# Block-sparse attention and MLP mixer on one core: the last batch's second MLP layer as seven block products

## The chip, the core and the metric

The kernel runs on one core of a Trainium2 chip. The metric is device time of one execution in microseconds: 278.38 us is the median of 9 runs of the kernel before (277.9 to 279.4). The work is shared between TensorE (PE, matrix products, with its weight loads shown as PEld), VectorE (DVE), ScalarE (ACT), GpSimd (POOL) and the DMA queues, of which SyncE (SP) issues most. The accumulators of PE lie in PSUM[...]; here they are handed out as "doubles", tiles of two banks.

## The reference, cut to what matters

For 4 batches of 768 rows, block-sparse attention of 8 heads of 64 gives x, and a mixer follows:

```
h = xt @ U @ V                      # over the sequence, rank 32
u = x + h.transpose(0, 2, 1)
ch = np.maximum(u @ w_ch1, 0.0) @ w_ch2
return (u + ch).astype(np.float32)
```

u is 768 x 512 for each batch, w_ch1 512 x 2048, w_ch2 2048 x 512. The change touches the last product, `@ w_ch2`, of the last batch alone.

## The kernel before, in words

The first batch's attention is done head pair by head pair. From then on a planner written into the kernel interleaves two streams for PE: attention units of the next batches (`try_unit`, `try_values`, `try_a`, `try_h`) and the MLP of a finished batch, held as a queue of small steps (`fill`, made by `mlp_steps(b)`, lines 717 to 888). The planner keeps a clock for each engine (`clk`), with durations written in by hand, and a list of tasks for ACT and DVE (`later`, `run_engines`). Nothing of it runs on the chip: it decides the order in which each engine's instructions stand, and each engine works its list strictly in that order, with semaphores between the engines.

For the last batch (b = 3) no attention is left to be interleaved. Its u, transposed (`uTs[b]`), comes from a chain for the last head pair: the values' product `pav`, DVE normalises it (`rcp`, `xs`, lines 588 and 590), POOL casts it (`xh`, 599), PE `pa`, DVE `a` (628, 629), PE `ph`, DVE `xf` (676), POOL `uh` (685), and a transposing DMA on SP (`uT`, 695). Meanwhile PE still works on the second layer of batch 2 (`w2_rows`), which DVE adds to `xf` and sends (`leave`, 792 and 795).

Then the last batch's MLP runs alone:

- **First layer** (`w1`, line 771). For each of 16 blocks jj of 128 hidden channels, 8 matmuls of 384 columns fill one double `pt`, and ACT's ReLU (line 737) writes it as fp16 into the tile `tT[jj]` (128 channels x 768 positions).
- **Second layer** (`w2`, line 826). For each of 6 row tiles sc, 16 matmuls of 512 columns accumulate over jj; stationary is `tT[jj][:, sc*128:...]`, moving is `w2t[:, jj, :]`. The last row tile is cut in columns 0 to 383 and 384 to 511. `leave` adds the bank to `xf` on DVE into a tile `of`, and SP sends it.

Positions are laid out with the six row tiles t as p*6+t, so "upper half" below means row tiles 0 to 2 and "lower half" 3 to 5. `double()` (line 114) gives out the double that comes free first; from line 1140 on there are four (numbers 0 to 3). Every matmul is issued at line 173 (`mm`).

Of the kernel before, what the change touches and what calls it, by code (L numbers as in the profile page):

```python
# [10 lines left out]
FP32 = mybir.dt.float32  # L11
FP16 = mybir.dt.float16
# [9 lines left out]
def kernel(  # L22
# [91 lines left out]
    def double(name, n=None):  # L114
        if n is None:
            n = min(doubles, key=lambda n: doubles[n][1])
            assert doubles[n][1] < OPEN
            clk["pe"] = max(clk["pe"], doubles[n][1])
        pool = doubles[n][0]
        t = pool.tile([P, 2, 512], FP32, tag=f"double{n}", name=name)  # L120
        doubles[n] = (pool, OPEN)
        held[id(t)] = (n, t)
        return t

    def give_back(t, when):
        n = held.pop(id(t))[0]
        doubles[n] = (doubles[n][0], when + LAG)
# [6 lines left out]
    def later(eng, first, fn, when=None):  # L134
        count[0] += 1
        when = clk["pe"] if when is None else when
        tasks[eng].append((when + LAG, first, count[0], fn))

    def run_engines(t):
        while True:  # L140
            best = None
            for eng in ("act", "dve"):
                for kind in (eng, "any"):
                    for task in tasks[kind]:
                        start = max(clk[eng], task[0])
                        late = 0.15 if kind == "any" and eng == "dve" else 0.0
                        key = (start + late, task[1], task[2])
                        if start <= t and (best is None or key < best[0]):
                            best = (key, eng, kind, task, start)
            if best is None:  # L150
                return
            _, eng, kind, task, start = best
            tasks[kind].remove(task)
            clk[eng] = start
            clk[eng] += task[3](eng)

    def more_doubles(tag, n):
        first[tag].__exit__(None, None, None)
        pool = ctx.enter_context(
            tc.tile_pool(  # L160
                name=f"double{n}p", bufs=1, space=bass.MemoryType.PSUM,
                side="left" if tag == "ps" else "right",
            )
        )
        doubles[n] = (pool, clk["pe"])

    def run_on(eng, us, ready=None):
        clk[eng] = max(clk[eng], (clk["pe"] if ready is None else ready) + LAG) + us
# [2 lines left out]
    def mm(out, lhsT, rhs, start, stop, loose=False, us=0.0):  # L171
        clk["pe"] += us
        ins = nc.tensor.matmul(  # L173
            out, lhsT, rhs, start=start, stop=stop, skip_group_check=loose
        )
        keep(ins)
        return ins
# [536 lines left out]
        run_on("dve", 0.6)  # L714


    def mlp_steps(b):
        tT = {}
        steps = []
# [5 lines left out]
        def relu(tiles, pt):  # L725
            if tiles[0][0] == tiles[1][0]:
                outs = [(tile_of(tiles[0][0]).rearrange("p (c n) -> p c n", c=2), pt[:, :, 0:HS])]
            else:
                outs = [
                    (tile_of(jj)[:, c * HS : (c + 1) * HS], pt[:, n, 0:HS])  # L730
                    for n, (jj, c) in enumerate(tiles)
                ]

            def run(eng):
                for o, i in outs:
                    if eng == "act":
                        keep(nc.scalar.activation(out=o, in_=i, func=AF.Relu))  # L737
                    else:
                        keep(nc.vector.tensor_scalar_max(out=o, in0=i, scalar1=0.0))  # L739
                us = {"act": 0.81, "dve": 0.95}[eng] + 0.16 * (len(outs) - 1)  # L740
                give_back(pt, clk[eng] + us)
                return us

            later("any", 1, run)

        def tile_of(jj):
            if jj not in tT:
                tT[jj] = tpool.tile([P, S], FP16, tag="tT", name="tT")
            return tT[jj]

        def w1_rows(key, tiles, phase, cc0=0, cc1=NCC):

# [32 lines left out]
        def leave(sc, nsc, n0, n1, pch, whole):  # L785
            if sc % 2 == 0 and n0 == 0:
                pair["of"] = opool.tile([P, 2, HD], FP32, tag="of", name="of")
            of = pair["of"][:, sc % 2 : sc % 2 + nsc, n0:n1]

            def run(eng):  # L790
                keep(
                    nc.vector.tensor_add(out=of, in0=xfs[b][:, sc : sc + nsc, n0:n1], in1=pch)  # L792
                )
                keep(
                    nc.sync.dma_start(
                        out=out[b].rearrange("(p t) d -> p t d", t=T)[:, sc : sc + nsc, n0:n1],
                        in_=of,
                    )
                )
                us = 0.1 + 0.55 * nsc  # L800
                give_back(whole, clk["dve"] + us)
                return us

            later("dve", 2, run)
# [18 lines left out]
            if phase == 1 and part == 7:  # L823
                leave(s0, 2, 0, HD, pair["pch"], pair["pch"])

        def w2(sc, part, n0, n1):
            if part == 0:
                pair["pch"] = double("pch")
            pch = pair["pch"][:, 0:1, 0 : n1 - n0]
            for jj in range(4 * part, 4 * part + 4):  # L830
                mm(
                    pch[:, 0, :],
                    tT[jj][:, sc * P : (sc + 1) * P],
                    w2t[:, jj, n0:n1],
                    jj == 0, jj == NJJ - 1, us=0.217 * (n1 - n0) / HD,
                )
            if part == 3:
                leave(sc, 1, n0, n1, pch, pair["pch"])

        rowed = b < B - 1  # L840
        if b == 0:

            first = [[(2 * k, 0), (2 * k + 1, 0)] for k in range(2)]
            for k, phase, cc0 in (
# [8 lines left out]
                        "",  # L853
                    )
                )
        for jj in range(NJJ):
            tiles = [(jj, 0), (jj, 1)]
            if b == 0 and jj < 4:
                if jj % 2:
                    continue  # L860
                tiles = [(jj, 1), (jj + 1, 1)]
            for ph in range(2):
                if rowed:
                    fn = lambda jj=jj, tiles=tiles, ph=ph: w1_rows(jj, tiles, ph)
                else:
                    fn = lambda jj=jj, ph=ph: w1(jj, ph)
                kind = "open" if ph == 0 else "swap" if rowed else ""
                steps.append((0.65, fn, kind))
        if rowed:
# [5 lines left out]
                            (0.434, lambda s0=s0, ph=ph, part=part: w2_rows(s0, ph, part), kind)  # L875
                        )
            return steps
        for sc in range(T):
            for n0, n1 in [(0, HD)] if sc < T - 1 else [(0, 384), (384, HD)]:
                for part in range(4):  # L880
                    steps.append(
                        (
                            0.87 * (n1 - n0) / HD,
                            lambda sc=sc, part=part, n0=n0, n1=n1: w2(sc, part, n0, n1),
                            "" if part else "open",
                        )
                    )
        return steps

    def start_batch(b):  # L890
# [190 lines left out]
    def next_unit(held_back=False):  # L1081
        i, u = stream.popleft()
        est = new_est()
        ests_of.setdefault(i, []).append(est)
        state["out"] += 1

        def mask(eng):
            us = mask_mul(u, est)
            masked.setdefault(i, []).append(clk["dve"] + us)
            return us  # L1090

        if held_back:
            scores(i, u, est)
            early.append(mask)
        else:
            scores(i, u, est, mask)
        unit_sides(i, u)
# [86 lines left out]
    def rate():  # L1184
# [4 lines left out]
            return max(left - 11.0, 0.0) / units if units else 1.2  # L1189
        return max(left - 12.9, 0.0) / max(units, 1)  # L1190

    def try_unit(due):
        if not stream or state["out"] > 12 or not free_double():
            return False
        if clk["act"] > clk["pe"] + (0.36 if due else 1.0) or due and credit < rate():
            return False
        next_unit()
        return True

    def try_fill():  # L1200
# [9 lines left out]
    while stream or fill or do_v or do_a or do_h or opened < B:  # L1210
        run_engines(clk["pe"])
        if not fill and opened < B and len(uT_at[opened]) == HP:
            if max(uT_at[opened]) <= clk["pe"]:
                fill.extend(mlp_steps(opened))
                opened += 1
        if try_h() or try_a() or try_values():
            continue
        if try_unit(True):
            credit -= rate()
            continue  # L1220
        if try_fill():

            weight = 0.87 if fill[0][0] > 0.5 else 1.24
            credit = min(credit + weight * run_fill(), 3.0)
            continue
        if try_unit(False):
            credit -= rate()
            continue
        clk["pe"] += 0.05
# [31 lines left out]
```

The softmax here doesn't subtract the row's maximum and nothing guards it: scores larger than these inputs give would overflow.

## Time and profile before

| | before |
|---|---|
| median of 9 runs | 278.38 us |
| the profiled execution, its own time | 278.47 us |
| its span in the profile | 276.7 us |
| PE busy | 270.7 us (98%) |
| DVE / ACT / POOL busy | 175.2 / 177.0 / 103.2 us |
| last batch, first layer on PE | 232.10 to about 252.9 us |
| last batch, second layer on PE | 252.91 to 273.83 us |
| last DVE addition starts | 273.88 us |

The span is what lies between the first and the last instruction of the profiled execution; its own time is 1.77 us longer. In the timeline view each row is a group of like instructions: start, duration, engine, line, operation, tile written and tiles read, shape, count, and in brackets the idle time of the engine before it with what ended it. Matmuls of one group overlap in the array, so the distance from one to the next is the group's duration less one instruction's mean, divided by the count less one. In the windows view each row is a stretch of time with the busy time of each engine in it, the granted TensorE clock (1.00 is full), the busy share of DMA and the GB/s.

### The profile page before, as it was taken

How to read it: one execution, taken by the hardware profiler on the slowest of the kernel's cores; microseconds unless marked ns; L12 is line 12 of the kernel's file. 1: busy time of each engine (PE TensorE's matmuls, PEld its weight loads, DVE VectorE, ACT ScalarE, POOL GpSimd, SP SyncE). 2: the span in 40 equal slices, each digit the busy share in tenths (PEclk: the TensorE clock that was granted, in tenths of full speed). 3: DMA queues.
4: the chain of work that ended last, by engine and by line, in shares of the span. 5: the costliest groups of instructions: out<-in, count | busy, mean ns of one | idle time of the engine just before them, and what ended most of it. 6: DMA issues, size and time to landing. Idle time of an engine off the chain costs nothing.

```text
span 276.7 us, 8037 instructions
## 1 busy us (share of the span) xinstructions
PE 270.7 (98%) x3493; PEld 161.9 (59%) x3493; DVE 175.2 (63%) x286; ACT 177.0 (64%) x198; POOL 103.2 (37%) x137
## 2 busy tenths in 40 slices
PE   8999999999999999999999999999999999999995
PEld 2677775565656564656565565656565654655443
DVE  6777758878797987777756768777777451000112
ACT  4899995877897857694955749584886201664000
POOL 4768639407274835363604536361102020000000
PEclk9999999999999999999999999999999999999999
DMA  6999957999979999995990989995100322000222
GB/s 192 310 297 263 281 136 104 182 181 77 136 48 118 168 121 145 155 108 71 49 123 0 189 91 161 136 98 75 31 2 2 104 79 81 25 1 0 78 77 76
DMA packets 85484, 31.65 MB, mean 114 GB/s; under 512 B 75152, under 2 KB 83048, under 8 KB 85448
## 3 DMA queue, kind: packets, MB, share of 16 engines
q0 software_dynamic: 49824, 10.29, 43.0%
q1 hardware_dynamic: 35268, 20.62, 33.4%
q8 instruction: 27, 0.44, 0.7%
q10 hardware_dynamic: 356, 0.22, 0.3%
q14 instruction: 9, 0.07, 0.1%
HBM read 27.84 MB, written 6.29 MB: 123 GB/s over the span
## 4 chain that ended last, share of the span: by engine, by line
PE 82%; ACT 11%; DMA 2%; DVE 1%; POOL 1%; issue 1%; SPq 0%; DVEq 0%; POOLq 0%
PE pch L173 30%; PE pt L173 30%; ACT est L499 11%; PE pav L173 10%; PE psc L173 9%; DMA kld<-in_k_dram 2%; PE pa L173 2%; PE ph L173 1%; POOL xh L599 0%; DVE xh L542 0%; DVE xs L590 0%; POOL qst L247 0%; POOL kst L327 0%; PE puT L704 0%; DVE uT L713 0%
## 5 line engine op out<-in xcount | busy, mean ns | idle before, releaser
L499 ACT ACTIVATE est<-psc 128x1024 f16<-128x1024 f32 x144 | 143.0, 1028 | 46.0 <-PE psc L173 44.6
L173 PE MATMUL pt<-uT,w1t 64*128 64x384 f16 (+1 forms) x896 | 94.4, 324 | 0.0
L173 PE MATMUL pch<-w2t,tT 64*128 64x512 f16 (+3 forms) x688 | 93.6, 372 | 0.1
L520 DVE TENSOR_TENSOR est<-est,m 128x1024 f16<-128x1024 f16 x108 | 78.3, 740 | 18.2 <-ACT est L499 16.8
L173 PEld LDWEIGHTS <-w1t 64*128 64x128 f16 (+1 forms) x896 | 46.0, 95 | 36.2 <-PE pt L173 8.4
L173 PEld LDWEIGHTS <-tT 64*128 64x128 f16 (+1 forms) x688 | 38.2, 95 | 36.9 <-PE pch L173 1.6
L737 ACT ACTIVATE tT<-pt 128x768 f16<-128x768 f32 (+1 forms) x48 | 36.6, 773 | 26.0 <-PE pt L173 26.0
L173 PEld LDWEIGHTS <-est 128*128 128x128 f16 x1152 | 41.4, 97 | 10.9 <-issue 5.0
L173 PE MATMUL pav<-vt,est 128*128 128x65 f16 x1152 | 44.5, 193 | 0.1
L792 DVE TENSOR_TENSOR of<-xf,pch 128x1024 f32<-128x1024 f32 (+3 forms) x16 | 15.2, 950 | 42.7 <-PE pch L173 42.7
L173 PE MATMUL psc<-qT,kT 64*128 64x512 f16 (+1 forms) x288 | 40.6, 323 | 0.3 <-ACT est L499 0.3
L599 POOL CAST xh<-xs 128x768 f16<-128x768 f32 x12 | 10.4, 870 | 79.8 <-DVE xs L590 74.2
L685 POOL CAST uh<-xf 128x768 f16<-128x768 f32 x12 | 13.9, 1161 | 26.1 <-DVE xf L676 14.5
L173 PE MATMUL psc<-qa,ka 128*128 128x512 f16 (+1 forms) x96 | 21.5, 326 | 0.6 <-ACT est L499 0.4
L739 DVE TENSOR_SCALAR tT<-pt 128x768 f16<-128x768 f32 (+1 forms) x20 | 18.3, 917 | 5.9 <-PE pt L173 5.8
L173 PEld LDWEIGHTS <-kT 64*128 64x128 f16 x288 | 14.6, 94 | 12.5 <-issue 0.7
L261 POOL DMA_DIRECT2D vt<-in_v_dram x20 | 16.3, 820 | 3.1 <-DMA w2t<-in_moe_w_ch_dram 3.1
L261 POOL DMA_DIRECT2D qst<-in_q_dram x20 | 16.3, 819 | 0.1
L261 POOL DMA_DIRECT2D kst<-in_k_dram x20 | 16.3, 820 | 0.0
L590 DVE TENSOR_TENSOR xs<-pav,rcp 128x768 f32<-128x768 f32 x12 | 11.5, 958 | 1.2
L676 DVE TENSOR_TENSOR xf<-xs,ph 128x768 f32<-128x768 f32 x12 | 11.4, 951 | 1.2 <-PE ph L173 1.2
L173 PEld LDWEIGHTS <-ka 128*128 128x128 f16 (+1 forms) x108 | 8.8, 97 | 3.6 <-issue 1.8
(70 smaller groups left out, 130.8 us busy)
## 6 DMA issues: line engine op xcount, KB each, us to landing
out_dram<-of SPq DMA_DIRECT2D x9, 512.0 KB, 3.3
vld<-in_v_dram SPq DMA_DIRECT2D x6, 384.0 KB, 7.2
w1t<-in_moe_w_ch_dram POOLq DMA_DIRECT2D x4, 512.0 KB, 9.0
w2t<-in_moe_w_ch_dram POOLq DMA_DIRECT2D x4, 512.0 KB, 10.0
qld<-in_q_dram SPq DMA_DIRECT2D x5, 384.0 KB, 6.6
kld<-in_k_dram SPq DMA_DIRECT2D x5, 384.0 KB, 8.0
qst<-in_q_dram POOLq DMA_DIRECT2D x20, 96.0 KB, 4.2
kst<-in_k_dram POOLq DMA_DIRECT2D x20, 96.0 KB, 4.4
```

What stands on the lines that cost most here:

```text
L173: ins = nc.tensor.matmul(out, lhsT, rhs, start=start, stop=stop, skip_group_check=loose)
L261: keep(nc.gpsimd.dma_start(out=o[:, h], in_=src_of(nm, i)[:, h]))
L499: keep(nc.scalar.activation(out=est, in_=psc, func=AF.Exp, scale=0.125))
L520: keep(nc.vector.tensor_tensor(out=o, in0=o, in1=m, op=ALU.mult))
L590: nc.vector.tensor_tensor(out=xs.rearrange("p (c j) (h d) -> p c (j h) d", c=2, h=2), in0=pv[:, :, :, 0:D], in1=rcp[:, :, :, None].broadca ...
L599: keep(nc.gpsimd.tensor_copy(out=xh, in_=xs))
L676: nc.vector.tensor_tensor(out=u.rearrange("p (c j) n -> p c j n", c=2), in0=xs.rearrange("p (c j) n -> p c j n", c=2), in1=ph[:, :, 0:HS]. ...
L685: keep(nc.gpsimd.tensor_copy(out=uh, in_=u))
L737: keep(nc.scalar.activation(out=o, in_=i, func=AF.Relu))
L739: keep(nc.vector.tensor_scalar_max(out=o, in0=i, scalar1=0.0))
L792: nc.vector.tensor_add(out=of, in0=xfs[b][:, sc : sc + nsc, n0:n1], in1=pch)
```

## The change

The second layer of the last batch becomes a Strassen product. The hidden activations t (768 x 2048) are cut in four blocks by upper and lower half of the positions and by jj 0 to 7 and 8 to 15; w_ch2 is cut by the same jj and by columns 0 to 255 and 256 to 511. With A the blocks of t and B those of w_ch2:

```
P1=(A11+A22)(B11+B22)  P2=(A21+A22)B11  P3=A11(B12-B22)  P4=A22(B21-B11)
P5=(A11+A12)B22        P6=(A21-A11)(B11+B12)             P7=(A12-A22)(B21+B22)
C12 = P5+P3    C21 = P2+P4    C22 = P1-P2+P3+P6    C11 = P1+P4-P5+P7
```

For each of three groups g of 128 positions in either half, each product is 8 matmuls of 256 columns.

- **Weight sums** (`add_w2`): ten DVE additions in fp16, five of 128x1536 and five of 128x512, put into the lists of DVE as soon as the last attention unit is issued, with the lowest priority (9). They are written into old load tiles and into `qa`.
- **Activation sums** (`add_t`): after the ReLU of jj+8, four DVE operations in fp16 (one of 768, three of 384 elements), eight times. Two of the four write in place over `tT`. The order of the first layer is changed to jj = 0, 8, 1, 9, ...
- **PSUM**: before the last batch's MLP is queued, doubles 2 and 3 are given up and become four tiles of one bank (`split_double`). The first layer is left with doubles 0 and 1.
- **Products** (`w2_product`): order P3, P5, P4, P2, P1, P6, P7. P3 and P5 fill the halves of tile `pa`, P4 and P2 those of `pb`, P1 lies in `pc`. P6 is accumulated onto P3, and P7 onto P4, after DVE has read P3 and P4 once. In the last group P7 is cut in two pieces of 128 columns, the second in `pd`.
- **Leaving**: DVE adds into `xf` in place, in pieces of 256 columns (three additions for `pa`, three for `pb`, one of 2x256 for `pc`, one each for P6 and P7 in a group), and SP sends 11 pieces of 128x256 and two of 128x128 in place of five of 128x512, one of 128x384 and one of 128x128.

How the planner orders this in the built program: on DVE four weight sums stand ahead of the last head pair's `rcp`, three between `xs` and `a`, and three behind `xf`; the last pair's `pa` stands 4 matmuls of the second layer of batch 2 later, and its `ph` 12 later. All 16 ReLUs of the last batch stay on ACT. First-layer tiles alternate between doubles 1 and 0; in every group `pa` is taken in double 1, `pb` in double 0, `pc` in one and the same single bank, and in the last group `pd` in a second; two single banks stay unused. The lists of ACT and POOL are the same as before; that of SP differs only in the output pieces.

The core of the diff:

```diff
+    def bank(name):
+        free = [(at, n) for n, (_, at) in banks.items()]
+        free += [(at + 0.1, n) for n, (_, at) in doubles.items()]
+        at, n = min(free, key=lambda f: (max(f[0], clk["pe"]), str(f[1])))
...
+            for o, i0, i1, op in (
+                (both, lo, hi, ALU.add),
+                (diag, lo[:, 0:HS], hi[:, HS:S], ALU.add),
+                (lo[:, HS:S], lo[:, HS:S], lo[:, 0:HS], ALU.subtract),
+                (hi[:, 0:HS], hi[:, 0:HS], hi[:, HS:S], ALU.subtract),
+            ):
+                keep(nc.vector.tensor_tensor(out=o, in0=i0, in1=i1, op=op))
...
+        def w2_product(g, n, j0, j1, n0=0, n1=HB):
+            where = {3: ("a", 0), 5: ("a", HB), 4: ("b", 0), 2: ("b", HB), 1: ("c", 0),
+                     6: ("a", 0), 7: ("b", 0)}
...
+                mm(
+                    o, t_sum[n, j][:, g * P : (g + 1) * P], w[:, n0:n1],
+                    fresh and j == 0, j == NJ - 1, True, us=0.108 * (n1 - n0) / HB,
+                )
...
+                if n == 5:
+                    acc(c11, pt[:, HB:512], ALU.subtract)
+                    acc(c12, pt[:, HB:512])
+                    acc(c12, pt[:, 0:HB])
+                    send(c12)
+                    done.add("a")
...
-        def w2(sc, part, n0, n1):
-            if part == 0:
-                pair["pch"] = double("pch")
-            pch = pair["pch"][:, 0:1, 0 : n1 - n0]
-            for jj in range(4 * part, 4 * part + 4):
-                mm(
-                    pch[:, 0, :],
-                    tT[jj][:, sc * P : (sc + 1) * P],
-                    w2t[:, jj, n0:n1],
-                    jj == 0, jj == NJJ - 1, us=0.217 * (n1 - n0) / HD,
-                )
-            if part == 3:
-                leave(sc, 1, n0, n1, pch, pair["pch"])
...
+        for g in range(3):
+            for n in (3, 5, 4, 2, 1, 6, 7):
+                for n0, n1 in [(0, HB)] if (g, n) != (2, 7) else [(0, P), (P, HB)]:
+                    for j0 in range(0, NJ, 4):
...
+                if opened == B - 1:
+                    while max(doubles[n][1] for n in (2, 3)) >= OPEN:
+                        clk["pe"] += 0.05
+                        run_engines(clk["pe"])
+                    for n in (2, 3):
+                        split_double(n)
```

More of the change, by code (lines that the diff above doesn't have):

```diff
@@ L158, in more_doubles @@
         first[tag].__exit__(None, None, None)
-        pool = ctx.enter_context(
+        closing[n] = ctx.enter_context(ExitStack())
+        pool = closing[n].enter_context(
             tc.tile_pool(
@@ L165, in more_doubles, with split_double, bank_back @@
         doubles[n] = (pool, clk["pe"])
+    closing, banks = {}, {}
+    def split_double(n):
+        assert doubles[n][1] < OPEN
+        at = doubles.pop(n)[1]
+        closing[n].close()
+        pool = ctx.enter_context(
+            tc.tile_pool(
+                name=f"bank{n}p", bufs=1, space=bass.MemoryType.PSUM,
+                side="left" if n == 3 else "right",
+            )
+        )
+        for m in range(2):
+            banks[f"bank{n}{m}"] = (pool, at)
+    def bank(name):
+        free = [(at, n) for n, (_, at) in banks.items()]
+        free += [(at + 0.1, n) for n, (_, at) in doubles.items()]
+        at, n = min(free, key=lambda f: (max(f[0], clk["pe"]), str(f[1])))
+        while min(banks.get(n, doubles.get(n))[1], OPEN) == OPEN:
+            clk["pe"] += 0.05
+            run_engines(clk["pe"])
+            free = [(at, n) for n, (_, at) in banks.items()]
+            free += [(at + 0.1, n) for n, (_, at) in doubles.items()]
+            at, n = min(free, key=lambda f: (max(f[0], clk["pe"]), str(f[1])))
+        if n in doubles:
+            clk["pe"] = max(clk["pe"], doubles[n][1])
+            return double(name, n)[:, 0, :], n
+        pool, at = banks[n]
+        clk["pe"] = max(clk["pe"], at)
+        banks[n] = (pool, OPEN)
+        return pool.tile([P, 512], FP32, tag=n, name=name), n
+    def bank_back(n, when):
+        if n in doubles:
+            for k in [k for k, v in held.items() if v[0] == n]:
+                del held[k]
+            doubles[n] = (doubles[n][0], when + LAG)
+        else:
+            banks[n] = (banks[n][0], when + LAG)
     def run_on(eng, us, ready=None):
@@ L714, in turn_u_pe, with w2_block, add_w2 @@
         run_on("dve", 0.6)
+    NJ, HB = NJJ // 2, HD // 2
+    W_SUMS = {
+        "11+22": (0, 0, 1, 1, ALU.add),
+        "12-22": (0, 1, 1, 1, ALU.subtract),
+        "21-11": (1, 0, 0, 0, ALU.subtract),
+        "11+12": (0, 0, 0, 1, ALU.add),
+        "21+22": (1, 0, 1, 1, ALU.add),
+    }
+    w_sum = {}
+    def w2_block(x, y, j0, j1):
+        return w2t[:, x * NJ + j0 : x * NJ + j1, y * HB : (y + 1) * HB]
+    def add_w2(n):
+        k, part = n // 2, n % 2
+        key = list(W_SUMS)[k]
+        x0, y0, x1, y1, op = W_SUMS[key]
+        if n == 0:
+            for m in range(6):
+                t = ldpool.tile([P, 6, HB], FP16, tag="ld" + "qkv"[m % 3], name="w2s")
+                w_sum["home", m] = t
+        j0, j1 = ((0, 6), (6, NJ))[part]
+        if part == 0:
+            o = w_sum["home", k][:, 0:6, :]
+        elif k < 3:
+            o = w_sum["home", 5][:, 2 * k : 2 * k + 2, :]
+        else:
+            o = qa[0][k - 3].rearrange("p (j n) -> p j n", n=HB)[:, 0:2, :]
+        keep(
+            nc.vector.tensor_tensor(
+                out=o, in0=w2_block(x0, y0, j0, j1), in1=w2_block(x1, y1, j0, j1), op=op
+            )
+        )
+        for j in range(j0, j1):
+            w_sum[key, j] = o[:, j - j0, :]
+        return 1.12 if part == 0 else 0.42
     def mlp_steps(b):
@@ L741, in run @@
                 give_back(pt, clk[eng] + us)
+                if not rowed:
+                    jj = tiles[0][0]
+                    full.add(jj)
+                    if (jj + NJ) % NJJ in full:
+                        later("dve", 1, lambda e: add_t(jj % NJ), clk[eng] + us)
                 return us
@@ L749, in tile_of, with add_t @@
             return tT[jj]
+        rowed = b < B - 1
+        full, t_sum, added = set(), {}, set()
+        def add_t(j):
+            lo, hi = tT[j], tT[NJ + j]
+            if j % 2 == 0:
+                t_sum["two"] = new_est().rearrange("p a n -> p (a n)")
+            both = new_est().rearrange("p a n -> p (a n)")[:, 0:S]
+            diag = t_sum["two"][:, (j % 2) * HS : (j % 2 + 1) * HS]
+            for o, i0, i1, op in (
[5 more added lines that the diff above has]
+                keep(nc.vector.tensor_tensor(out=o, in0=i0, in1=i1, op=op))
+            t_sum[1, j] = diag
+            t_sum[2, j] = both[:, HS:S]
+            t_sum[3, j] = lo[:, 0:HS]
+            t_sum[4, j] = hi[:, HS:S]
+            t_sum[5, j] = both[:, 0:HS]
+            t_sum[6, j] = lo[:, HS:S]
+            t_sum[7, j] = hi[:, 0:HS]
+            added.add(j)
+            return 1.5
@@ new lines, in force, with acc, send, run @@
+        def force(done):
+            while not done():
+                clk["pe"] += 0.05
+                run_engines(clk["pe"])
+        def w2_product(g, n, j0, j1, n0=0, n1=HB):
+            where = {3: ("a", 0), 5: ("a", HB), 4: ("b", 0), 2: ("b", HB), 1: ("c", 0),
+                     6: ("a", 0), 7: ("b", 0)}
+            nm, at = where[n] if n0 == 0 else ("d", 0)
+            fresh = n in (3, 4, 1) or nm == "d"
+            if j0 == 0:
+                if fresh:
+                    pair[nm, g] = bank("p" + nm)
+                if n == 3:
+                    pair["done", g] = set()
+            done = pair["done", g]
+            if n in (6, 7) and j0 == 0 and nm != "d":
+                force(lambda: nm in done)
+            o = pair[nm, g][0][:, at : at + n1 - n0]
+            for j in range(j0, j1):
+                force(lambda: j in added and ("21+22", NJ - 1) in w_sum)
+                w = {
+                    1: lambda: w_sum["11+22", j],
+                    2: lambda: w2_block(0, 0, j, j + 1)[:, 0, :],
+                    3: lambda: w_sum["12-22", j],
+                    4: lambda: w_sum["21-11", j],
+                    5: lambda: w2_block(1, 1, j, j + 1)[:, 0, :],
+                    6: lambda: w_sum["11+12", j],
+                    7: lambda: w_sum["21+22", j],
+                }[n]()
+                mm(
+                    o, t_sum[n, j][:, g * P : (g + 1) * P], w[:, n0:n1],
+                    fresh and j == 0, j == NJ - 1, True, us=0.108 * (n1 - n0) / HB,
+                )
+            if j1 < NJ:
+                return
+            last = g == 2
+            xq = xfs[b].rearrange("p t (c n) -> p (t c) n", c=2)
+            c11, c12, c21, c22 = 2 * g, 2 * g + 1, 2 * g + 6, 2 * g + 7
+            def acc(q, i, op=ALU.add, n0=0, n1=HB):
+                o = xq[:, q, n0:n1]
+                keep(nc.vector.tensor_tensor(out=o, in0=o, in1=i, op=op))
+            def send(q, n0=0, n1=HB):
+                t, c = divmod(q, 2)
+                keep(
+                    nc.sync.dma_start(
+                        out=out[b].rearrange("(p t) d -> p t d", t=T)[
+                            :, t, c * HB + n0 : c * HB + n1
+                        ],
+                        in_=xq[:, q, n0:n1],
+                    )
+                )
+            pt, pn = pair[nm, g]
+            def run(eng):
+                us = 0.36
+                if n == 5:
[4 more added lines that the diff above has]
+                    done.add("a")
+                    us = 1.2
+                if n == 2:
+                    acc(c22, pt[:, HB:512], ALU.subtract)
+                    acc(c21, pt[:, HB:512])
+                    if last:
+                        acc(c11, pt[:, P:HB], n0=P)
+                    acc(c21, pt[:, 0:HB])
+                    send(c21)
+                    done.add("b")
+                    us = 1.4 if last else 1.2
+                if n == 1:
+                    o = xq[:, c11 : c22 + 1 : c22 - c11, :]
+                    i = pt[:, None, 0:HB].broadcast_to([P, 2, HB])
+                    keep(nc.vector.tensor_tensor(out=o, in0=o, in1=i, op=ALU.add))
+                    us = 0.68
+                if n == 6:
+                    acc(c22, pt[:, 0:HB])
+                    send(c22)
+                if n == 7:
+                    acc(c11, pt[:, 0 : n1 - n0], n0=n0, n1=n1)
+                    send(c11, n0, n1)
+                if n in (1, 6, 7):
+                    bank_back(pn, clk["dve"] + us)
+                return us
+            if n in (5, 2, 1, 6, 7):
+                later("dve", 2, run)
@@ L824, in w2_rows @@
                 leave(s0, 2, 0, HD, pair["pch"], pair["pch"])
-        def w2(sc, part, n0, n1):
-            if part == 0:
-                pair["pch"] = double("pch")
-            pch = pair["pch"][:, 0:1, 0 : n1 - n0]
-            for jj in range(4 * part, 4 * part + 4):
-                mm(
-                    pch[:, 0, :],
-                    tT[jj][:, sc * P : (sc + 1) * P],
-                    w2t[:, jj, n0:n1],
-                    jj == 0, jj == NJJ - 1, us=0.217 * (n1 - n0) / HD,
-                )
-            if part == 3:
-                leave(sc, 1, n0, n1, pch, pair["pch"])
-        rowed = b < B - 1
         if b == 0:
@@ L855, in mlp_steps @@
                 )
-        for jj in range(NJJ):
+        for jj in range(NJJ) if rowed else [j + x * NJ for j in range(NJ) for x in range(2)]:
             tiles = [(jj, 0), (jj, 1)]
@@ L877, in mlp_steps @@
             return steps
[L878 to L885, printed above, removed]
+        for g in range(3):
+            for n in (3, 5, 4, 2, 1, 6, 7):
+                for n0, n1 in [(0, HB)] if (g, n) != (2, 7) else [(0, P), (P, HB)]:
+                    for j0 in range(0, NJ, 4):
+                        steps.append(
+                            (
+                                0.434 * (n1 - n0) / HB,
+                                lambda g=g, n=n, j0=j0, n0=n0, n1=n1: w2_product(
+                                    g, n, j0, j0 + 4, n0, n1
+                                ),
+                                "",
+                            )
                         )
-                    )
         return steps
@@ L1190, in rate, with add_w2_soon @@
         return max(left - 12.9, 0.0) / max(units, 1)
+    def add_w2_soon():
+        for n in range(10):
+            later("dve", 9, lambda eng, n=n: add_w2(n))
     def try_unit(due):
@@ L1197, in try_unit @@
         next_unit()
+        if not stream:
+            add_w2_soon()
         return True
@@ L1213 @@
             if max(uT_at[opened]) <= clk["pe"]:
+                if opened == B - 1:
+                    while max(doubles[n][1] for n in (2, 3)) >= OPEN:
+                        clk["pe"] += 0.05
+                        run_engines(clk["pe"])
+                    for n in (2, 3):
+                        split_double(n)
                 fill.extend(mlp_steps(opened))
```

## The prediction

> **What bounds the kernel now.** I read the page first, then the windows view of the end, then its timeline.
>
> ```profile
> PE 82%; ACT 11%; DMA 2%; DVE 1%; POOL 1%; issue 1%; SPq 0%; DVEq 0%; POOLq 0%
> PEclk9999999999999999999999999999999999999999
> ```
>
> 82% of the chain of waits is PE, and the clock is full in every slice, so a matmul column costs the same everywhere. The windows show the last batch:
>
> ```profile
> 240.00:245.00 5.00, 5.00 (x33) 3.00 (x32) 0.00 (x0) 3.24 (x4) 0.00 (x0) 1.00 0.01 2
> 255.00:260.00 5.00, 5.00 (x25) 2.25 (x23) 0.69 (x1) 0.00 (x0) 0.00 (x0) 1.00 0.15 56
> 265.00:270.00 5.00, 5.00 (x25) 2.28 (x24) 0.69 (x1) 0.00 (x0) 0.00 (x0) 1.00 0.29 107
> ```
>
> PE (first figure) is busy without a gap, DVE (third) idle in the first layer and 14% busy in the second. What shortens PE's stream here shortens the kernel, as long as DVE, which gets the sums, keeps up. The timeline gives the stages:
>
> ```profile
> 220.88 2.76 PE L173 MATMUL pch<-w2t,tT 64*128 64x512 f16 x24
> 232.10 20.98 PE L173 MATMUL pt<-uT,w1t 128*128 128x384 f16 x128
> 252.91 20.92 PE L173 MATMUL pch<-w2t,tT 128*128 128x512 f16 x112
> 253.18 0.81 ACT L737 ACTIVATE tT<-pt 128x768 f16<-128x768 f32 x1 [0.55 <-PE pt L173]
> 273.88 0.29 DVE L792 TENSOR_TENSOR of<-xf,pch 128x128 f32<-128x128 f32 x1 [0.34 <-PE pch L173]
> ```
>
> **Matmuls: the gain.** The second layer is 80 matmuls of 512 columns, 16 of 384, 16 of 128; it becomes 160 of 256 and 16 of 128. Their spacing, from groups of one shape in the timeline (group's duration less one mean, over count less one): six of 512 in 1.46 us with mean 379 ns, 0.216; the 128 first-layer matmuls of 384, 0.163; the 16 of 128 in 1.06 us with mean 219, 0.056; and for 256 columns over all 128 rows the nearest row is an early score group:
>
> ```profile
> 23.04 0.60 PE L173 MATMUL psc<-qa,ka 128*128 128x256 f16 x4
> ```
>
> with mean 271 ns: (0.60 - 0.27) / 3 = 0.109. Before: 80 x 0.216 + 16 x 0.163 + 16 x 0.056 = 20.8. After: 160 x 0.1085 + 0.9 = 18.25. **Gain 2.6 us.**
>
> The Trainium skill ("TensorE: Matmul & The Clock Gate", Back-to-back issue gap) speaks against it: in a stream of weight load and matmul pairs it gives about 81 ns at 128 columns and 131 at 512, so narrow matmuls cost more per column. An estimate on the line between these is 98 for 256 columns and 114 for 384: before 80 x 131 + 16 x 114 + 16 x 81 = 13.6 us, after 160 x 98 + 16 x 81 = 17.0, a loss of 3.4 us. The trace has 216 and 56 ns in place of 131 and 81, straight proportion to columns, though every matmul loads its own weights (98 ns mean, overlapping: 72 pairs of 65 columns pass in 2.44 us, 33 ns each). I take the trace; the page's direction is the slower rival.
>
> **Weight sums on DVE.** The masks show fp16 with both inputs in SBUF: 0.69 us for 1024 elements alone, two in 1.28, so one following at once costs 0.08 less. The fp32 additions (0.29 at 128 elements, 0.56 at 384, 0.69 at 512) start from 0.155; taking that start, an fp16 element costs (0.69 - 0.155) / 1024 = 0.52 ns. So 1536 elements cost 0.155 + 1536 x 0.52 ns = 0.95, 512 cost 0.42; all ten 6.9 us.
> - Four stand ahead of the last `rcp`. DVE was idle 3.52 us there (217.46 to 220.98); four take 0.95 + 0.34 + 0.87 + 0.34 = 2.5. Cost nothing; cover gone, they would delay `rcp` one for one.
> - Three stand behind `xs` (ends 222.28), beside POOL's cast `xh`. How the two meet:
>
> ```profile
> 213.21 1.91 DVE L520 TENSOR_TENSOR est<-est,m 128x1024 f16<-128x1024 f16 x2
> 213.42 1.17 POOL L685 CAST uh<-xf 128x768 f16<-128x768 f32 x1 [3.54 <-DVE xf L676]
> 227.09 0.83 POOL L685 CAST uh<-xf 128x768 f16<-128x768 f32 x1 [3.85 <-DVE xf L676]
> ```
>
>  One waits for the other: the cast grows by 0.34, and two masks take 1.91 instead of 1.28. So the first sum runs 222.2 to 223.15, `xh` then ends at 223.85 (was 223.24), the other two sums end at 224.1 and 225.0. PE's `pa` stands 4 matmuls later (0.108 each in the 64-row rows above), due at 223.9 instead of 223.48: stall 0 to 0.15, taken 0.1. `a` ends at 225.5 (was 224.64); `ph` stands 12 matmuls later, due at 226.1, so it doesn't wait. DVE's `of` then ends at 226.7 and `xf` at 227.5 (was 226.97).
> - Three stand behind `xf`, where POOL's `uh` waits for the first: ends 228.6 (was 227.92). The transposing DMA lands 2.7 us after issue: 231.3, was 230.65. First needed by the fourth first-layer matmul at 232.6. Cover 1.3 us.
>
> SP's output of batch 2 moves from 226.13 to 226.7 ahead of that transpose; nothing waits for SP in between.
>
> **First layer on two doubles.** ReLU starts 0.21 us after the next tile's first matmul (233.62 against 233.41), lasts 0.81, so the double is free at 234.43; two tiles on, it is wanted at 234.70. Fits with 0.27 to spare; a wait by semaphore costs 0.05 (`a` ends 224.64, `ph` starts 224.69). Only the second tile, in double 0, waits for DVE's last `of` of batch 2 (ends 233.44 against 233.41): 0.1.
>
> **Activation sums.** 0.555 for 768 elements, then 0.27, 0.39 (waits for its forerunner), 0.27: 1.5 us for each pair of tiles, which PE takes 2.6 for. Hidden, but for the last: ReLU 15 ends at 253.99, its sum of 768 at 254.6, and P5's eighth matmul is due at 254.54: 0.1. All eight weight loads of P5's first group carry a wait; satisfied ones cost between 0 and 0.05 each (0.4 in all). Four consecutive first-layer matmuls with a wait each, at 232.1 to 232.6, keep their 0.163; I take 0.
>
> **Products and DVE.** 256 elements out of PSUM are 0.42. `pa`: 0.42 + 0.34 + 0.45 = 1.2; `pb` the same, 1.35 in the last group; `pc` 0.69; P6 and P7 0.42 each: 3.9 us a group against PE's 56 x 0.1085 = 6.08. The points where PE waits, counted from the group's start: P6 needs `pa` read (1.74 + 0.2 + 1.2 = 3.1, due 4.34); P7 needs `pb` (3.67 + 1.2 = 4.9, due 5.2). The next group's P3 goes into the same double as P6, since doubles are preferred while two banks lie unused: `pc` is added till 5.5, P6 till 5.95, the wait makes 6.0, wanted at 6.08. It fits by under 0.1, twice (first group: late `add_t` ends at 255.5, same margin). I take 0.1 for both together.
>
> **Tail.** Before, the last DMA is issued 0.57 us after the last matmul starts (273.62, 274.19), with DVE free. Now DVE is still behind with `pc` and P6 when P7's halves end: last addition ends 0.55 after the last matmul starts, and SP, 0.33 us for each of three issues in a row, starts the last one 0.88 after. Lost: 0.3. Bounds 0 (DVE as quick as the matmuls) and 0.7 (each of three 64 to 128 KB pieces lands behind the other; alone they took 1.6 to 2.0).
>
> **Sum.** -2.6 + 0.1 (`pa`) + 0.1 (`of`) + 0.1 (P5) + 0.1 (P3) + 0.3 (tail) + 0.1 (three DMAs landing together) = -1.8. The profiled execution took 278.47 (span 276.7 and 1.77 around it): 276.7. The median shown lies 0.09 lower: **276.6**.
>
> **Rivals.**
> - *PE waits at the group's edge.* The margin at P3 is under 0.1. If DVE's nine additions a group run 0.3 longer than summed, they take each of two edges 0.25 and the tail 0.3: 277.4. For it: six hand-offs in a row with no such chain in the trace; against: each duration has a row. 18%.
> - *POOL is shut out.* If DVE's sums, issued back to back, keep the port between them, `xh` waits for all three (225.2), PE stalls 1.3 at `pa`, and `uT` comes 0.2 late: 278.1, no change. The skill ("SBUF — State Buffer", Who interferes with whom) has the port locked for one whole instruction, loser blocked; against the rival, a cast at 68.45 took 1.18 beside two masks issued back to back, so POOL came in between. 6%.
> - *Slower: weight loads show.* A load lasts 98 ns and a 256-column matmul 108; the trace has only runs of four such. If in runs of 160 the load isn't hidden, a pair costs the load and the 33 ns of a bare pair, 131 ns: 160 x 0.0225 = 3.6 more, 280.2. It decides from 120 ns on (1.8 / 160 = 11 ns). Against: 65-column pairs at 33 ns. 10%.
>
> The change does what it says: the products are in PE's list, 56 a group.
>
> **Chances.** My sum 66% (276.0 to 277.1), rivals 18, 6, 10. The range 276.0 to 277.9 takes in the first rival and half the second. A measurement of this kernel tells 0.2% (0.56 us) from no change: faster 0.83 (sum and nearly all of the first rival), same 0.07, slower 0.10.
>
> **What would show it.** P matmuls 0.108 apart and 18.3 us from P3 to P7's end; `uT` landing before 232; first-layer tiles 1.30 apart; `pa` free before each group starts; three DMA issues 0.35 apart at the end. Wrong if 256-column matmuls stand 0.12 or more apart, if a group lasts over 6.3, or if the first layer starts after 232.6.

## The result and the profile after

The changed kernel takes **276.83 us** (median of 16 runs) against 278.69 us for the kernel before in the same measurement: a ratio of 0.9931, 95% interval 0.9918 to 0.9944. Run twice more beside other kernels on later occasions it gave 0.9957 (0.9945 to 0.9969) and 0.9939 (0.9917 to 0.9961). It is faster each time, by 1.2 to 1.9 us. The prediction was 276.6 us, range 276.0 to 277.9.

The trace shown below is of the second measurement, since the first profiled execution, one of the 16, took 342.32 us at a granted TensorE clock of 0.76 (the ratio leaves it out) and can't be compared with the trace of before. The span of the trace shown is 275.5 us and its own time 277.31. First the page: the chain of waits and the clock.

```profile
PEclk9999999999999999999999999999999999999999
...
PE 92%; DVE 2%; ACT 2%; DMA 1%; POOL 0%; issue 0%; SPq 0%; DVEq 0%; POOLq 0%
```

The clock is full as before, and PE is still what the end waits for. Then the windows view of the last batch, with the same columns as before:

```profile
240.00:245.00 5.00, 5.00 (x33) 2.99 (x32) 2.47 (x8) 3.04 (x5) 0.00 (x0) 1.00 0.00 2
255.00:260.00 5.00, 5.00 (x48) 4.32 (x46) 4.33 (x13) 0.00 (x0) 0.00 (x0) 1.00 0.17 56
265.00:270.00 5.00, 5.00 (x48) 4.48 (x46) 2.70 (x8) 0.00 (x0) 0.00 (x0) 1.00 0.24 84
```

DVE, idle in the first layer before, is now half busy there, and in the first group of products it is busy for 4.33 of 5 us. PE has 48 matmuls where it had 25 and shows no gap in these windows.

The traces don't start alike: the last head pair's `pav` begins at 218.49 in the trace of before and between 218.2 and 219.1 in those of the runs below, after identical instructions on PE. So I count from that point. Before, then after, with the last row that PE works on:

```profile
218.49 2.45 PE L173 MATMUL pav<-vt,est 128*128 128x65 f16 x72
273.62 0.22 PE L173 MATMUL pch<-w2t,tT 128*128 128x128 f16 x1
```

```profile
219.09 2.45 PE L217 MATMUL pav<-vt,est 128*128 128x65 f16 x72
271.90 0.28 PE L217 MATMUL pd<-qa,tT 128*128 128x128 f16 x2
```

The last row holds two matmuls, and the second starts at 271.96. From `pav` the last matmul starts after 55.13 us before and 52.87 us after, and the span ends after 58.18 and 56.44: **1.74 us saved**. Two more traces with the same order of instructions (the third measurement, and the one of all banks below) give 56.45 and 56.46. Of the kernel before there is one trace; up to the second layer the run with matmuls of 256 columns repeats it (first layer 13.61 us after `pav`, lasting 20.81, in both). The three traces of the changed order differ by up to 0.9 us ahead of `pav` and by 0.02 us behind it. So the scatter of the measured ratios is likely from the part ahead, which the change leaves alone, but only the traced executions show it. Which mean is right stays open at some 0.3 us.

### The profile page after: what moved, and what is told of

Same layout as the page of the kernel before. It is cut to its first block, busy times and chain, and to the rows that moved or that the text cites. A ratio compares the mean times of both kernels' runs of the same rounds, so it can differ in the third digit from the quotient of the medians.

```text
span 340.5 us, 8244 instructions
## 1 busy us (share of the span) xinstructions
PE 335.9 (99%) x3557; PEld 193.3 (57%) x3557; DVE 201.6 (59%) x350; ACT 182.0 (53%) x198; POOL 103.4 (30%) x137
## 4 chain that ended last, share of the span: by engine, by line
PE 98%; ACT 1%; DVE 0%; issue 0%
PE pt L217 32%; PE pch L217 24%; PE psc L217 15%; PE pav L217 13%; PE pa L217 5%; PE pb L217 3%; PE pturn L310 1%; PE warm L217 1%; PE ph L217 1%; PE pc L217 1%; ACT est L543 1%; PE pmk L217 0%; PE puT L756 0%; PE pm L217 0%; PE pd L217 0%; PE puT L748 0%
## 5 line engine op out<-in xcount | busy, mean ns | idle before, releaser
L217 PE MATMUL pt<-uT,w1t 64*128 64x384 f16 (+1 forms) x896 | 120.0, 388 | 0.0
L217 PE MATMUL pch<-w2t,tT 64*128 64x512 f16 x576 | 92.3, 457 | 0.1
L217 PEld LDWEIGHTS <-w1t 64*128 64x128 f16 (+1 forms) x896 | 54.3, 108 | 50.6 <-PE pt L217 9.9
L217 PEld LDWEIGHTS <-tT 64*128 64x128 f16 (+1 forms) x680 | 41.6, 107 | 42.4 <-issue 34.5
L217 PEld LDWEIGHTS <-est 128*128 128x128 f16 x1224 | 55.8, 104 | 16.8 <-issue 12.7
L217 PE MATMUL pav<-vt,est 128*128 128x65 f16 x1152 | 50.7, 204 | 0.0
L217 PE MATMUL psc<-qT,kT 64*128 64x512 f16 (+1 forms) x288 | 48.6, 384 | 0.1
L217 PE MATMUL psc<-qa,ka 128*128 128x512 f16 (+1 forms) x96 | 26.5, 388 | 0.1
L857 DVE TENSOR_TENSOR est<-tT 128x768 f16<-128x768 f16 (+1 forms) x16 | 6.6, 454 | 17.4 <-ACT tT L822 17.4
L1003 DVE TENSOR_TENSOR of<-xf,pch 128x1024 f32<-128x1024 f32 x9 | 11.0, 1217 | 6.7 <-PE pch L217 6.7
```

The costliest lines, as they stand in the source:

```text
L217: ins = nc.tensor.matmul(out, lhsT, rhs, start=start, stop=stop, skip_group_check=loose)
L857: keep(nc.vector.tensor_tensor(out=o, in0=i0, in1=i1, op=op))
```

## The experiments

**The changed kernel again.** No edit.

> The changed kernel unchanged, for a profile at full TensorE clock. My sum: ratio to before 0.993 to 0.994; in the profile 256-column matmuls 0.108 us apart, 18.3 us from the first matmul of P3 to the last of P7, waits of 0.1 us each at the last head pair's pa, at the second first-layer tile, in P5 of the first group and at the edges of the groups, and the last DMA issued 0.88 us after the last matmul starts (0.57 before). The rival of waits at the groups' edges: 0.25 us at each of two edges.

The ratio was 0.9957 (0.9945 to 0.9969), a little less gain than expected. The stages can be read off the timeline of this run. First two rows of the kernel before, then the chain to the transposed u and the start of the first layer after:

```profile
222.41 0.83 POOL L599 CAST xh<-xs 128x768 f16<-128x768 f32 x1 [7.83 <-DVE xs L590]
227.94 1.22 SPq L695 DMA_TRANSPOSE uT<-uh  x1
```

```profile
217.98 2.48 DVE L793 TENSOR_TENSOR w2s<-w2t 128x1536 f16<-128x1536 f16 x4
221.47 3.19 PE L217 MATMUL pch<-w2t,tT 64*128 64x512 f16 x28
221.58 0.23 DVE L632 RECIPROCAL rcp<-pav 128x12 f32<-128x12 f32 x1 [1.12 <-PE pav L217]
...
222.79 2.78 DVE L793 TENSOR_TENSOR w2s<-w2t 128x1536 f16<-128x1536 f16 x3
223.00 1.42 POOL L643 CAST xh<-xs 128x768 f16<-128x768 f32 x1 [7.83 <-DVE xs L634]
...
224.50 0.50 PE L217 MATMUL pa<-xh,Ut 64*128 64x128 f16 x12
...
229.13 1.21 SPq L739 DMA_TRANSPOSE uT<-uh  x1
...
232.68 21.05 PE L217 MATMUL pt<-uT,w1t 128*128 128x384 f16 x128
```

The four sums ahead of `rcp` take 2.48 us and leave DVE idle for 1.12: they cost nothing. POOL's cast `xh` took 0.83 us before and takes 1.42 beside the next three: it waits 0.6 us for the first sum, as the prediction had it. It ends at 224.42, and PE, which has 28 matmuls to do ahead of `pa` and not 24, begins `pa` at 224.50 without a gap. `uT`'s transposing DMA is issued at 229.13, 0.6 us later from `pav` than before, and 2.7 us later it has landed: 231.8, with the fourth first-layer matmul at 233.2. The first layer starts 13.59 us after `pav` as against 13.61: the detour of the weight sums is wholly hidden.

The end of the same timeline:

```profile
253.56 1.04 PE L217 MATMUL pa<-w2s,tT 128*128 128x256 f16 x8
...
254.67 0.83 DVE L857 TENSOR_TENSOR est<-tT 128x768 f16<-128x768 f16 x2 [1.24 <-ACT tT L822]
255.28 0.10 PEld L217 LDWEIGHTS <-est 128*128 128x128 f16 x1 [0.20 <-DVE est L857]
...
259.25 0.42 DVE L911 TENSOR_TENSOR xf<-xf,pa 128x256 f32<-128x256 f32 x1
...
259.77 1.04 PE L217 MATMUL pa<-w2s,tT 128*128 128x256 f16 x8
...
265.88 1.04 PE L217 MATMUL pa<-w2s,tT 128*128 128x256 f16 x8
```

The weight load for P5's eighth matmul waits for the last activation sum; the matmul comes 0.08 us late. At the edge of the first group P6 has been added by 259.25 + 0.42 = 259.67, and the next group's P3 starts at 259.77. The margin is 0.1 us. The third group's P3 starts at 265.88, so the second group's 56 matmuls take 6.11 us, 0.109 each; the first group takes 6.21, which is 0.1 more for the wait in P5. No wait at an edge is left to find.

**Before, with matmuls of 256 columns.**

```diff
-            for n0, n1 in [(0, HD)] if sc < T - 1 else [(0, 384), (384, HD)]:
+            for n0, n1 in [(0, 256), (256, HD)] if sc < T - 1 else [(0, 256), (256, 384), (384, HD)]:
```

> The kernel before with the last batch's second layer in matmuls of 256 columns (192 in place of 80 of 512 and 16 of 384, the last piece cut 256, 128, 128), no block products. The theory that cost is in proportion to columns: the same time as before within 0.2% (5 x 32 x 0.1085 + 16 x 0.1085 + 32 x 0.056 = 20.9 us, as the 20.8 before). The rival that weight loads show at 256 columns: 176 x 0.0225 = 4 us slower, ratio 1.014.

The ratio was 1.0012 (1.0003 to 1.0022): no more than 0.6 us slower, where the rival had 4. The timeline:

```profile
253.15 21.16 PE L173 MATMUL pch<-w2t,tT 128*128 128x256 f16 x208
```

176 matmuls of 256 and 32 of 128 columns (merged into one row under the first shape) in 21.16 us, where 112 wider ones took 20.92. Weight loads of 98 ns stay hidden behind matmuls of 256 columns in a long run too. Single matmuls of 256 columns in this trace stand 0.1092 us apart. The 0.1085 in my sums was too low: the row of four early matmuls that it was to come from gives 0.109. For 176 matmuls that is the 0.1 us more than my sum for this kernel.

**All banks in turn.**

```diff
-        at, n = min(free, key=lambda f: (max(f[0], clk["pe"]), str(f[1])))
+        at, n = min(free, key=lambda f: (max(f[0], clk["pe"]), f[0], str(f[1])))
```

> The changed kernel, but each product tile takes the place that has been free longest, so that all four single banks and both doubles are used in turn and P3 of a group no longer waits for P6 of the group before to be added. The order of instructions is the same. My sum puts 0.1 us on these waits for both edges together: 0.0 to 0.2 us faster than the changed kernel. The rival of waits at the edges: 0.5 us or more faster.

From `pav` to the last matmul it takes 52.87 us, as the changed kernel; to the end 56.46 (56.44). From the first group's P3 to the second's it is 6.21 us, as above:

```profile
252.74 1.04 PE L217 MATMUL pa<-w2s,tT 128*128 128x256 f16 x8
...
258.95 1.04 PE L217 MATMUL pa<-w2s,tT 128*128 128x256 f16 x8
```

Its ratio to before, 0.9948 (0.9935 to 0.9960), can't be told from the changed kernel's. The edges of the groups cost nothing, and the rival of waits there falls.

**Without the weight sums.** `add_w2_soon()` isn't called, and plain blocks of w_ch2 stand in for the five sums.

```diff
-                    1: lambda: w_sum["11+22", j],
+                    1: lambda: w2_block(0, 0, j, j + 1)[:, 0, :],
...
-        if not stream:
-            add_w2_soon()
```

> The changed kernel without the ten weight sums on DVE; P1, P3, P4, P6 and P7 take a plain block of w_ch2 in place of a sum, so the output is another product. My sum: the weight sums cost 0.1 us at the last head pair's pa and nothing else, so 0.1 us faster than the changed kernel, and the transposed u lands 0.65 us earlier. The rival that POOL or the chain to the transposed u is held up by the sums: 1 us or more faster, with the first layer's first matmul that much earlier.

The ratio was 0.9941 (0.9927 to 0.9956). Counted from `pav`, the first layer starts after 13.61 us (13.59 with the sums), the last matmul after 52.81 (52.87), the end comes after 56.40 (56.44):

```profile
222.90 0.83 POOL L643 CAST xh<-xs 128x768 f16<-128x768 f32 x1 [7.82 <-DVE xs L634]
223.96 0.50 PE L217 MATMUL pa<-xh,Ut 64*128 64x128 f16 x12
...
228.43 1.21 SPq L739 DMA_TRANSPOSE uT<-uh  x1
```

The cast is back at 0.83 us and the transpose 0.6 us earlier from `pav` (9.45 us; 10.04 with the sums), and no work of PE comes earlier for it; nothing is won at `pa`, where 0.1 us was expected. Two things differ besides the sums. The planner puts `pa` and `ph` back to their places of before (24 matmuls stand ahead of `pa`, not 28). And the second first-layer tile starts 1.31 us after the first, not 1.38, although DVE's `of` ends 1.33 us after the start of the first layer in both traces: the tile no longer waits for that addition, which points to another double. These 0.07 us cover all that is won, and they are not time that the sums take.

**Each weight sum twice.** The cover was tested with a double dose.

```diff
-        keep(
-            nc.vector.tensor_tensor(
-                out=o, in0=w2_block(x0, y0, j0, j1), in1=w2_block(x1, y1, j0, j1), op=op
+        for _ in range(2):
+            keep(
+                nc.vector.tensor_tensor(
+                    out=o, in0=w2_block(x0, y0, j0, j1), in1=w2_block(x1, y1, j0, j1), op=op
```

> The changed kernel with each of the ten weight sums issued twice at its place on DVE; the order of all else is kept. If the sums cost nothing because they lie in DVE's idle time and in the slack of the chain to the transposed u, that cover has an end. My sum for the doubled list: eight sums take 5.0 us against 3.6 us from the end of the masks to rcp, so rcp comes 1.4 us late; PE waits 1.5 us at the last head pair's pa and 1.5 us at its ph; the transposed u still lands in time. Together 3.0 us slower than the changed kernel (2.5 to 3.5). If the sums ran beside the chain at no cost whatever their number: no change.

It took 280.6 us where the changed kernel took 276.81 in the same measurement, 3.8 us more (ratio to before 1.0074, 1.0045 to 1.0103), and more than the 2.5 to 3.5 expected; the first layer starts 3.6 us later from `pav`.

```profile
217.32 5.38 DVE L794 TENSOR_TENSOR w2s<-w2t 128x1536 f16<-128x1536 f16 x8
...
222.62 0.23 DVE L632 RECIPROCAL rcp<-pav 128x12 f32<-128x12 f32 x1
...
223.82 5.10 DVE L794 TENSOR_TENSOR w2s<-w2t 128x1536 f16<-128x1536 f16 x6
224.04 1.42 POOL L643 CAST xh<-xs 128x768 f16<-128x768 f32 x1 [9.52 <-DVE xs L634]
225.51 0.51 PE L217 MATMUL pa<-xh,Ut 64*128 64x128 f16 x12 [1.51 <-POOL xh L643]
...
229.51 0.34 PE L217 MATMUL ph<-a,Vd 64*128 64x128 f16 x6 [1.76 <-DVE a L673]
```

The idle time in brackets is where PE waits, by 1.51 and 1.76 us, and it does so at the two places expected. Counted from `pav`, `pa` starts 1.67 us later than in the changed kernel, `ph` and then the first layer 3.6. Eight sums take 5.38 us and not 5.0: the second of two sums into the same tile starts 0.03 us after the first has ended, while sums into different tiles start 0.08 before. That is what the expectation left out.

In the row of six, POOL gets its cast in after the first sum: 1.42 us again. But here too the second sum stands 0.03 us behind the first, so this run doesn't say what a longer list without such gaps would do. The better row is in the changed kernel's own trace, where the second of the three sums, of another tile, had started before the first had ended and then stood still for the cast:

```profile
223.65 1.04 DVE L793 TENSOR_TENSOR w2s<-w2t 128x512 f16<-128x512 f16 x1
```

It took 1.04 us where such a sum takes 0.41 alone. So two sums issued back to back don't shut POOL out. The weight sums are free because the idle time and the slack that they lie in are long enough for them; for twice as many they are not.

**The last but one piece on ACT's queue.**

```diff
-                    send(c11, n0, n1)
+                    send(c11, n0, n1, nc.scalar if n1 == P else nc.sync)
```

> The changed kernel, but the last but one output piece (C11, columns 0 to 127 of the last group) is issued by ACT's queue, which is idle, so that SP has two pieces in a row and not three. If the tail's cost is SP's issue in a row: the last issue comes 0.3 us earlier and the kernel ends 0.3 us earlier. If it is DVE's lag or the landing of the pieces together: no change.

First the last two issues of the kernel before in the timeline, then the changed kernel's last microseconds, then this run's:

```profile
273.56 0.96 SPq L795 DMA_DIRECT2D out_dram<-of  x2
```

```profile
271.89 0.28 DVE L911 TENSOR_TENSOR xf<-xf,pb 128x128 f32<-128x128 f32 x1
271.90 0.28 PE L217 MATMUL pd<-qa,tT 128*128 128x128 f16 x2
272.00 1.30 SPq L916 DMA_DIRECT2D out_dram<-xf  x3
272.21 0.29 DVE L911 TENSOR_TENSOR xf<-xf,pd 128x128 f32<-128x128 f32 x1
```

```profile
271.20 0.86 SPq L916 DMA_DIRECT2D out_dram<-xf  x2
271.40 0.36 ACTq L916 DMA_DIRECT2D out_dram<-xf  x1
271.41 0.29 DVE L911 TENSOR_TENSOR xf<-xf,pd 128x128 f32<-128x128 f32 x1
```

In the changed kernel SP needs 1.30 us for three issues, and the last stands 0.40 us behind the addition that it sends (272.90 against 272.50). Here it follows that addition by 0.03. From the last matmul's start to the end of the span it is 3.25 us in place of 3.57, so 0.32 us come back, as expected.

The last addition ends 0.55 us after the last matmul's start in all three traces (before: 273.88 + 0.29 against 273.62), so DVE isn't late for the last piece. And 0.2 us of the tail stay: the last issue starts 0.57 us after the last matmul's start in this run as in the kernel before (273.56 + 0.96 - 0.33 = 274.19), but the end comes 0.2 later. The traces split that. The last piece lands 1.63 us after its issue (1.56 before). And at the end SP waits for the semaphores of its transfers one after another: here two such waits, already satisfied, stand behind the one for the last piece (0.06 us each), in the kernel before none. The ratio was 0.9928 (0.9902 to 0.9955); beside the changed kernel's 0.9939 of the same measurement the intervals can't tell the two apart.

**Order, banks and queue together.** The edits of the two runs above for queue and banks, and one more:

```diff
-            for n in (3, 5, 4, 2, 1, 6, 7):
+            for n in (3, 5, 4, 2, 1, 6, 7) if g else (3, 4, 5, 2, 1, 6, 7):
```

> The changed kernel with three edits: the output piece on ACT's queue as in the run before, every product tile in the place that has been free longest, and in the first group the order P3, P4, P5, P2, so that P5's last weight load comes after the last activation sum. Expected: no wait in P5 (0.08 us in the profile of the changed kernel), with the queue's 0.3 together 0.4 us faster than the changed kernel.

The wait in P5 is gone; one of 0.03 us appears at the first group's P7. From `pav` to the end it takes 56.04 us, 0.4 less than the changed kernel, as expected. Its 276.42 us (ratio 0.9921, 0.9895 to 0.9947) are the lowest median of all kernels run; against the changed kernel's 276.81 only the traces, not the intervals, show it ahead.

**The changed kernel a third time.**

> The changed kernel unchanged once more, beside the runs of this call, since its two ratios so far are 0.9931 and 0.9957. The profile puts the gain at 1.8 us: ratio 0.9935.

The ratio was 0.9939 (0.9917 to 0.9961), in agreement.

## Why the prediction was right, point by point

The sum was -1.8 us, and the trace shows -1.74 from the last head pair on. Its terms, with what the trace of the second measurement has:

| Term | predicted, us | measured, us | seen in |
|---|---|---|---|
| second layer's matmuls | -2.6 | -2.39 | last matmul's start less first's: 20.71 before, 18.40 less P5's wait after |
| PE waits at the last pair's `pa` | +0.1 | 0 | first layer starts at the same time from `pav` |
| second first-layer tile waits for `of` | +0.1 | +0.07 | first layer 20.88, was 20.81 |
| P5 waits for the last activation sum | +0.1 | +0.08 | the waiting weight load |
| edges of the groups | +0.1 | 0 | no gap; all banks in turn changes nothing |
| tail, with the landing of three pieces | +0.4 | +0.5 | last matmul's start to the span's end: 3.05 before, 3.57 after |

That the sum comes within 0.06 us is partly luck: the gain and the tail came out 0.3 worse than put down, and the four small waits 0.25 better. What the runs bear out is the mechanism, that PE's matmuls set the time and nearly all of the extra work on DVE is covered.

- **Matmuls.** The gain is smaller by 0.2: half because 256-column matmuls stand 0.1092 us apart and not 0.1085 (160 x 0.0007 = 0.1), a figure that was below the 0.109 of its own row; the rest from rounding up 2.55 and from counting end to end. The trace's proportion to columns held (56 ns at 128 columns, 216 at 512). The figures of the Trainium skill ("TensorE: Matmul & The Clock Gate", Back-to-back issue gap) for a stream of pairs, 81 ns at 128 columns and 131 at 512, didn't. The run of 256 columns without block products rules out a loss of several microseconds.
- **Weight sums and the chain to `uT`.** Shown hidden by leaving them out; doubling them shows where the cover ends. The figures for `xh` and for the transpose's issue came out within 0.1 us of the sum. My 0.1 for a wait at `pa` was a hedge; the 4 matmuls put ahead of it cover it.
- **First layer on two doubles.** Tiles stay 1.30 us apart after the second. The 0.27 us to spare was enough.
- **Edges.** The sum said a fit by under 0.1, the trace has 0.1. The rival that had 18% falls: DVE's nine additions a group last as summed.
- **Tail.** SP's three issues in a row came as described, and the queue run shows that they are 0.32 of the 0.5. They stand 0.43 and 0.48 us apart, not 0.33, so the last starts 0.94 us after the last matmul's start and not 0.88. DVE's lag was no loss of its own: the last addition ends 0.55 us after the last matmul's start, as the sum said, but it did so before the change too. The 0.1 put down for the landing stands for 0.05 of later landing and 0.1 of SP's closing waits, which the sum didn't know of.

The measured 276.83 us is 0.2 above the forecast, well inside the scatter between measurements.

## What to carry to other kernels

When PE is the only engine with no gap, trade its work for work of engines that are idle in the same stage, and price each transfer of work by the wait that would appear: here some 7 us of weight sums on DVE were hidden, and twice as many cost 3.8 us, nearly all of it at two places known beforehand. In such an exchange the edges of the stage are what remains: the last sum ahead of the first product, and the last DMA issues, which stand in a row on one queue. Spread these over queues that have nothing else to do: here one piece moved gave 0.32 us in the trace.

## What the runs showed of the hardware

- A long stream of 256-column matmuls, each with its own weight load of 98 ns, runs at 0.109 us a pair, as the early runs of four did; the load adds nothing that the traces show.
- POOL's cast beside VectorE's sums of two SBUF inputs waits for the one in progress and then goes ahead of the next one, though that had been issued back to back: the cast took 1.42 us in place of 0.83, the sum that it overtook 1.04 in place of 0.41. A longer list without gaps was not run.
- Two VectorE sums into the same tile don't overlap: the second starts 0.03 us after the first has ended, against 0.08 before its end for sums into different tiles.
- A DMA issue on SP takes 0.33 us alone. The three last pieces started 0.43 and 0.48 us apart: a semaphore instruction stands between two issues (about 0.1 us with the gaps around it), and the second and third issue themselves took 0.38 and 0.40. Why these are longer stays open.
